# DeltaNet attention with a soft mixture of experts on one core: solved keys in feature-major form, the state product added to the solved values in PSUM, joins on 64-row tiles, 3 KB store rows, outputs transposed per step

## The chip, the cores and the metric

The kernel runs on one core of one Trainium2 chip. The metric is device time in microseconds (us), lower is better. The kernel before was timed three times: a median of 350.14 us, the lowest 349.73.

The engines are named as in the profile. PE is TensorE (matrix products and transposes), PEld its weight loads, DVE is VectorE, ACT is ScalarE, POOL is GpSimd, and SP is SyncE, which issues transfers only. A product of fp32 data appears as two matmul records, a transpose as one.

## The reference

There are 4 batches, 8 heads, 768 tokens and a head size of 48. The output of the delta rule is laid out as 3072 tokens of 384 features. It goes into a soft mixture of 8 experts with 4 slots each and a hidden size of 1024. All of it is fp32.

```python
k_n = k / (np.linalg.norm(k, axis=-1, keepdims=True) + 1e-06)
for t in range(S):
    y[:, :, t] = einsum('bhd,bhde->bhe', q[:, :, t], state)
    v_old = einsum('bhde,bhd->bhe', state, kt)
    state = state + bt[:, :, :, None] * einsum('bhd,bhe->bhde', kt, vt - v_old)
...
logits = x @ phi
d = exp(logits - logits.max(0));  d /= d.sum(0) + 1e-09
slot_input = d.T @ x
slot_out[e] = maximum(slot_input[e] @ w1[e], 0) @ w2[e]
c = exp(logits - logits.max(1));  c /= c.sum(1) + 1e-09
out = c @ slot_out
```

## The kernel before

The sequence is cut into 24 chunks of 32 tokens. The 4 batches times 32 tokens fill the 128 partitions, so one chunk covers all batches and heads. Four chunks make a group, of which there are six.

For each group, `invert(m)` builds the inverse of the 32 x 32 lower triangular matrix of every batch, head and chunk, scaled by beta and the key norms. DVE transposes the products of keys (`lb`, L509) and computes the norms (L524 to L540). The two diagonal 16 x 16 blocks are inverted by elimination (28 small steps, L558 and L562), on DVE for the first group and on POOL for the others. The off-diagonal block is joined by two series of small products on PE (X16, L601, and T16, L607). The result `DTb` is written in two copies masked by the parity of the batch.

For each chunk, `turn` transposes K and Q on PE (L446), and ACT copies the result to `X` (L455), keys in half 0 and queries in half 1. `products` forms K K' and Q K' (L473). They become `G` (for the inversion) and the masked `AT` (L494). `scale_v` multiplies V by the norms on POOL.

The recurrence is in `chain(n)`. It runs from the state St as follows:

- R: PE multiplies the keys with the state (L655), and DVE subtracts that from V into a tile R (L668).
- QS: PE multiplies the queries with the state (L655) into the bank of the output.
- W: PE applies the inverse to R (L678). DVE and ACT copy the solved values out in two masked halves (L689 and two at L694), and POOL adds the halves to `Wc` (L698).
- S: PE adds the update to the state, which stays in banks 6 and 7 (L706); ACT and DVE copy it to St (L716, L720).
- AU: PE multiplies AT with Wc and adds it to the output bank (L731); ACT copies it to Y (L737).

After each group, `route(m)` transposes the four chunks of Y (L755, one bank for each of three feature blocks), forms the logits, both softmaxes and the slot sums. After the last group, `experts()` forms the maximum over all tokens (L963), the slots' inputs (L981), the expert products (L1001 and L1039), and the output: 24 products of 384 columns (L1079), 12 copies of two banks each on DVE or ACT (L1086, L1089), and 48 stores with rows of 1.5 KB (L1096), from SP and ACT in turn. The weights are loaded into buffers of the recurrence as those become free.

The order of the work is written by `Plan` while the program is built. Each step is recorded with an engine, a cost, and what it reads and writes. `order()` then runs a list schedule by the longest remaining path and emits the steps engine by engine in that order. It counts the PSUM banks (six, of which four at most hold work outside the recurrence, kind "bulk") and puts products of the identity (fillers, `plan.fill`, L404) into gaps of PE. Each engine runs its instructions strictly in the emitted order. A transfer is issued by an instruction on SP, ACT or POOL and waits there until its buffer is free.

The constants are set before the first planned step: memsets of tS, Dn and St on POOL (L398 to L400), of the padding of K and Q on DVE (L397). The transfers of beta on POOL (L435) stand behind them.

Of the kernel before, what the change touches and what calls it, by code (L numbers as in the profile page):

```python
# [14 lines left out]

class Op:
    __slots__ = ("eng", "us", "fn", "deps", "succ", "acq", "rel", "bias", "land", "tail", "start", "end", "left", "at", "name", "area", "passes")
# [10 lines left out]
class Plan:  # L28
# [12 lines left out]
    WINDOW, KEEP, DENSE, BONUS, FORCE = 2.5, 0.46, 0.5, 40.0, 0.0  # L41

    def __init__(self, banks, limit):
# [3 lines left out]
        self.fill = None  # L47

    def op(self, eng, us, fn, r=(), w=(), acq=None, rel=None, pre=(), bias=0.0, land=0.0, name="", touch=None):
# [3 lines left out]
        o.eng, o.us, o.fn, o.acq, o.rel, o.bias, o.land, o.name = eng, us, fn, acq, rel, bias, land, name  # L53
# [50 lines left out]
    def order(self):  # L104
# [3 lines left out]
        clock, held = {}, {"bulk": 0, "chain": 0}  # L108
# [47 lines left out]
        while len(done) < n:  # L156
# [3 lines left out]
            for eng, ls in ready.items():  # L160
                now = clock.get(eng, 0.0)
                cand = []
                for t, o in ls:
# [10 lines left out]
                    if t is not None:  # L174
                        cand.append((t, o))
                if cand:
                    first = min(c[0] for c in cand)

                    def worth(c):
                        return c[1].tail + (bonus if eng == "PE" and c[1].area > self.DENSE * c[1].us  # L180
                                            else 0.0), -c[1].at
# [25 lines left out]
            if o.eng == "PE":  # L207
                idle = clock.get("PE", 0.0)
                while self.fill and idle >= self.fill[3] and (
# [8 lines left out]
                    f.eng, f.at, f.name, f.start = "PE", -1, "fill", idle  # L218
                    end = array(idle, self.fill[0], self.fill[1], 2)
                    f.us, idle, f.end = end - idle, end, end  # L220
                    t = max(t, idle)
                    done.append(f)
                    n += 1
                us = array(t, us, o.area, o.passes) - t
            o.start, o.end = t, t + us
# [27 lines left out]
def kernel(  # L253
# [16 lines left out]
    P = 128  # L270
# [32 lines left out]
    NK, NX, NV, NQ, NA = 11, 9, 7, 5, 9  # L303
# [10 lines left out]
    tt = buf([P, 2, QC, QC], "tt")  # L314
    pr = buf([P, 2 * 7 * 8], "pr")
    tS = buf([P, C, C], "tS")
    DT = buf([P, U, C], "DT")
    Gl = buf([P, U, QC], "Gl")
    DTb = ring(2, [P, U, 2, C], "DTb")
    tD, oD = buf([P, QC, 2, QC], "tD"), buf([P, U, QC], "oD")  # L320
    gmx = buf([P, 2, QC], "gmx")
    Dn = buf([P, U // 2, C], "Dn")
    X16 = buf([P, U // 2, 2, QC], "X16")
    R = buf([P, H, D], "R")
# [66 lines left out]
    nc.gpsimd.memset(low, -1.0)  # L391
    nc.gpsimd.affine_select(out=low, in_=low, compare_op=ALU.is_ge, fill=0.0, base=-1,
# [3 lines left out]
    for t in (Kall, Qall):  # L396
        nc.vector.memset(t.rearrange("p n (h d) -> p (n h) d", d=DP)[:, :, D:DP], 0.0)  # L397
# [762 lines left out]
```

## Time and profile before

| what | value |
|---|---|
| median of the runs | 350.14 us |
| the profiled execution's own time | 350.11 us |
| its span, first to last instruction | 348.3 us |
| instructions shown | 16203 |
| mean granted clock of TensorE | 0.931 |
| read from HBM, written | 39.47 MB, 4.72 MB |
| fillers (L404), matmul records | 232, 37.9 us busy |
| Wc on POOL (L698), 24 of 1002 ns | 24.0 us busy, 63.2 us idle ahead of it |
| key and query products with the state (L655), 1472 records | 37.5 us busy |
| solve (L678), 736 records on 64*64 tiles | 26.3 us busy |
| joins (L601 and L607), 768 records each on 32*32 tiles | 9.8 us busy each |

"Busy" is the time in which an engine had an instruction running. "Idle before" is the time it stood ahead of one, put down to what came last. PE's records overlap, so the mean of one record (220 ns for the solve) is longer than the distance from one to the next. The granted clock is the share of full speed that the throttle left to TensorE. All rows come from one execution, whose span is 1.8 us shorter than its own time.

### The profile page before, as it was taken

How to read it: one execution, taken by the hardware profiler on the slowest of the kernel's cores; microseconds unless marked ns; L12 is line 12 of the kernel's file. 1: busy time of each engine (PE TensorE's matmuls, PEld its weight loads, DVE VectorE, ACT ScalarE, POOL GpSimd, SP SyncE). 2: the span in 40 equal slices, each digit the busy share in tenths (PEclk: the TensorE clock that was granted, in tenths of full speed). 3: DMA queues.
4: the chain of work that ended last, by engine and by line, in shares of the span. 5: the costliest groups of instructions: out<-in, count | busy, mean ns of one | idle time of the engine just before them, and what ended most of it. 6: DMA issues, size and time to landing. Idle time of an engine off the chain costs nothing.

```text
span 348.3 us, 16203 instructions
## 1 busy us (share of the span) xinstructions
PE 278.8 (80%) x7182; PEld 222.1 (64%) x7182; DVE 178.4 (51%) x384; ACT 130.7 (38%) x258; POOL 132.0 (38%) x263
## 2 busy tenths in 40 slices
PE   2873096997959986898988878998787899999970
PEld 1762096886848776787867667886666787334430
DVE  7098919746561753836576484664642632210600
ACT  1321054543453625564436444453164434011050
POOL 9710401488128740289504891258811110000000
PEclk9987579998998999999899999999999999999955
DMA  6755643154445333324342405475458389697287
GB/s 120 134 85 91 100 67 59 28 88 81 75 106 86 66 55 70 66 49 77 52 80 77 111 10 145 110 193 164 135 173 332 104 272 307 212 389 282 75 259 208
DMA packets 90853, 45.24 MB, mean 130 GB/s; under 512 B 80400, under 2 KB 83600, under 8 KB 90784
## 3 DMA queue, kind: packets, MB, share of 16 engines
q1 hardware_dynamic: 74176, 39.15, 44.0%
q10 hardware_dynamic: 16064, 4.92, 6.5%
q8 instruction: 56, 0.92, 1.1%
q0 software_dynamic: 544, 0.15, 0.3%
q14 instruction: 13, 0.11, 0.1%
HBM read 39.47 MB, written 4.72 MB: 127 GB/s over the span
## 4 chain that ended last, share of the span: by engine, by line
PE 53%; POOL 17%; DVE 13%; issue 9%; DMA 3%; ACT 2%; SPq 0%; POOLq 0%; DVEq 0%; ACTq 0%
PE bank L655 6%; PE bank L731 6%; PE bank L446 5%; PE bank L678 5%; POOL tt L562 4%; PE bank L473 4%; POOL pr L558 4%; PE bank L404 4%; PE bank L1079 4%; PE bank L706 3%; PE bank L1039 3%; PE bank L1001 3%; POOL Wcall L698 3%; PE bank L601 3%; POOL bt L435 2%
## 5 line engine op out<-in xcount | busy, mean ns | idle before, releaser
L698 POOL TENSOR_TENSOR Wcall<-W 128x384 f32<-128x384 f32 x24 | 24.0, 1002 | 63.2 <-ACT W L694 59.1
L655 PE MATMUL bank<-St,X 128*32 128x96 f32 x1472 | 37.5, 248 | 8.6 <-issue 6.1
L455 ACT ACTIVATE X<-bank 128x1024 f32<-128x1024 f32 (+1 forms) x28 | 25.3, 902 | 42.2 <-PE bank L446 35.8
L404 PE MATMUL bank<-ident 128*128 128x128 f32 x232 | 37.9, 307 | 2.5 <-issue 2.5
L655 PEld LDWEIGHTS bank<-St,X 128*32 128x32 f32 x1472 | 31.1, 110 | 13.2 <-issue 8.8
L404 PEld LDWEIGHTS bank<-ident 128*128 128x128 f32 x232 | 32.8, 214 | 6.5 <-issue 4.8
L446 PE MATMUL bank<-ident,Kall 128*128 128x128 f32 x96 | 19.0, 331 | 20.9 <-DVE ATall L494 13.1
L473 PE MATMUL bank<-X 48*64 48x128 f32 (+1 forms) x896 | 28.4, 266 | 7.7 <-ACT X L455 3.4
L731 PE MATMUL bank<-Wcall,ATall 64*64 64x48 f32 x768 | 27.8, 221 | 8.3 <-POOL Wcall L698 6.9
L731 PEld LDWEIGHTS bank<-Wcall,ATall 64*64 64x64 f32 x768 | 24.8, 136 | 11.7 <-POOL Wcall L698 9.6
L694 ACT ACTIVATE W<-bank,par 128x192 f32<-128x192 f32 x48 | 17.6, 418 | 38.8 <-PE bank L678 28.4
L720 DVE TENSOR_TENSOR St<-bank,half 128x768 f32<-128x768 f32 x23 | 21.9, 952 | 19.3 <-PE bank L706 19.1
L473 PEld LDWEIGHTS bank<-X 48*64 48x64 f32 x896 | 23.3, 139 | 10.4 <-issue 5.1
L678 PE MATMUL bank<-R,DTb 64*64 64x48 f32 x736 | 26.3, 220 | 2.5 <-issue 1.4
L513 POOL TENSOR_TENSOR tt<-lb,low 128x256 f32<-128x256 f32 x12 | 8.5, 734 | 52.0 <-DVE lb L509 52.0
L446 PEld LDWEIGHTS bank<-ident,Kall 128*128 128x128 f32 x96 | 13.0, 168 | 24.0 <-DVE ATall L494 13.4
L678 PEld LDWEIGHTS bank<-R,DTb 64*64 64x64 f32 x736 | 23.6, 135 | 6.1 <-issue 3.6
L716 ACT ACTIVATE St<-bank 48x384 f32<-48x384 f32 x46 | 22.3, 484 | 13.3 <-PE bank L706 12.4
L562 POOL TENSOR_TENSOR tt<-tt,pr 128x28 f32<-128x28 f32 (+6 forms) x70 | 24.4, 348 | 5.5
L490 DVE SCALAR_TENSOR_TENSOR G<-bank,par,G 128x128 f32<-128x128 f32 x48 | 15.0, 344 | 20.8 <-ACT G L486 20.8
L558 POOL TENSOR_TENSOR pr<-tt 128x28 f32<-128x28 f32 (+6 forms) x70 | 23.7, 338 | 4.9
L689 DVE TENSOR_TENSOR W<-bank,par 128x384 f32<-128x384 f32 x24 | 13.3, 555 | 23.6 <-PE bank L678 23.4
(211 smaller groups left out, 533.6 us busy)
## 6 DMA issues: line engine op xcount, KB each, us to landing
Qall<-in_q_dram SPq DMA_DIRECT2D x96, 48.0 KB, 2.5
Kall<-in_k_dram SPq DMA_DIRECT2D x92, 48.0 KB, 2.4
X<-in_moe_w_dram SPq DMA_DIRECT2D x7, 512.0 KB, 4.2
X<-in_moe_w_dram SPq DMA_DIRECT2D x7, 384.0 KB, 6.4
Vall<-in_v_dram ACTq DMA_DIRECT2D x48, 48.0 KB, 2.7
Vall<-in_v_dram SPq DMA_DIRECT2D x48, 48.0 KB, 2.8
Kall<-in_moe_w_dram SPq DMA_DIRECT2D x4, 512.0 KB, 4.1
ATall<-in_moe_w_dram SPq DMA_DIRECT2D x3, 512.0 KB, 3.6
```

Source lines behind the costliest of these rows:

```text
L404: plan.fill = (0.223, 0.213, 0.1, 6.0, lambda b: nc.tensor.matmul(bank[:, b, 0:P], lhsT=ident, rhs=ident, start=True, stop=True, skip_grou ...
L446: nc.tensor.transpose(at(h, j)[:, P * e:P * e + P], src[:, P * e:P * e + P], ident)
L455: plan.op("ACT", act(512 * len(which)), lambda: nc.scalar.activation(dst, at(h, 0, 2) if len(which) > 1 else at(h).unsqueeze(1), ACT.Copy) ...
L473: nc.tensor.matmul(at(h, g)[rb, 2 * w * C * e:2 * w * C * (e + 1)], lhsT=x[r, 0, e, rb], rhs=x[r, which[0]:which[0] + w, e, rb], start=(e ...
L558: eng.tensor_tensor(o, t[:, :, j, 0:j].unsqueeze(2).broadcast_to([P, 2, w, j]), t[:, :, j + 1:QC, j].unsqueeze(3).broadcast_to([P, 2, w, j ...
L562: eng.tensor_tensor(t[:, :, j + 1:QC, 0:j], t[:, :, j + 1:QC, 0:j], o, op=ALU.add)
L655: nc.tensor.matmul(at(h)[rb, 2 * D * e:2 * D * e + 2 * D], lhsT=x[:, i, e, rb], rhs=St[:, b, e].rearrange("p g d -> p (g d)"), start=(e == ...
L678: nc.tensor.matmul(at(hw, u // HQ)[rb, D * (u % HQ):D * (u % HQ) + D], lhsT=t[rb, H * c + u].rearrange("p j t -> p (j t)"), rhs=rhs[rb, u, ...
L698: plan.op("POOL", pool(384), lambda: nc.gpsimd.tensor_tensor(wc, ww[:, :, 0, :], ww[:, :, 1, :], op=ALU.add), r=wk, w=[("Wc", n % 2)], nam ...
L716: plan.op("ACT", act(384), lambda r=r, g=g: nc.scalar.activation(St[r].rearrange("p (i j) e g d -> p i g (j e) d", i=2)[:, 0, g], bank[r, ...
L720: D_(dve(768, True), lambda: nc.vector.tensor_tensor(St.rearrange("p (i j) e g d -> p i (j e) g d", i=2)[:, 1], bank[:, SB + 1, 0:H * D].r ...
L731: nc.tensor.matmul(at(hy)[rb, D * u:D * u + D], lhsT=a[rb, u % 2, u // 2, :], rhs=wc[rb, u, :], start=(n == 0 and u == 0), stop=True, skip ...
```

## The change

The parts of the change, in the order of the kernel:

- Start: the memsets of tS, Dn, St, the padding and banks 6 and 7 become planned steps. Beta's transfers no longer stand behind them. All V loads are issued from SP instead of half of them from ACT. K has 10 ring slots instead of 11, V 6 instead of 7. The K half of `turn` and `products` stands apart from the Q half for the first three groups instead of the first.
- Inversion: the factor of the low triangle is formed from the norms (two DVE steps in place of two on POOL), tt has two buffers, and the norm is one step shorter (a factor of 2 is carried into V, a factor of 4 into beta, and taken out of Y by 0.5). The joins run as 32 products on 64-row tiles instead of 64 on 32-row tiles. For that Gl and Dn are written in two copies masked by parity (Gl by two ACT copies, Dn by two POOL steps).
- Recurrence: PE multiplies the inverse with the keys (KP), in feature-major form, and ACT copies it negated over the keys in X. VP applies the inverse to V itself. R multiplies the solved keys with the state and adds that to VP's result in the same banks. The subtraction on DVE and the tile R are gone. Wc is copied from PSUM by ACT instead of added on POOL.
- Routing: Y is transposed per chunk, three blocks into one bank.
- Output: cT is laid out by pairs of tokens, so that an output row in SBUF holds two neighbouring tokens (3 KB). 48 products of 64 rows replace 24 of 128. There are 24 stores; 18 are issued by SP, 6 by ACT. Four pairs of banks are used in turn, the last being the state's.
- Plan: a table of 150 priorities by engine and step, start times of the engines, and a cost for changing the tile shape on PE.

```diff
-    NK, NX, NV, NQ, NA = 11, 9, 7, 5, 9
+    NK, NX, NV, NQ, NA = 10, 9, 6, 5, 9
...
-        load(v, V[n % NV], ("V", n % NV), n, ("SP", "ACT"), [("V", n % NV)])
+        load(v, V[n % NV], ("V", n % NV), n, ("SP",), [("V", n % NV)])
...
+        for j in (1, 0):
+            plan.op("POOL", 0.72, lambda j=j: nc.gpsimd.tensor_tensor(
+                Dn[:, :, j, 0:QC], Dn[:, :, 0, 0:QC],
+                par[:, j:j + 1].unsqueeze(2).broadcast_to([P, U // 2, QC]), op=ALU.mult),
+                r=[kn], w=[kn], name="Dn2")
...
-        def couple(qs, first):
-            for q2 in qs:
-                for b in range(B):
-                    r = slice(C * b, C * b + C)
+        def couple(first):
+            for q2 in range(U // 2):
+                for i in range(2):
+                    r = slice(2 * C * i, 2 * C * i + 2 * C)
...
-            plan.op("PE", pe(16, 32, 96, 4, 0.25), lambda: state(hr, 0),
-                    r=[("X", n % NX, 0)] + sk, w=[hr], acq=hr, name="R")
-            D_(dve(384, True), lambda: nc.vector.tensor_tensor(
-                R.rearrange("p u d -> p (u d)"), vn.rearrange("p u d -> p (u d)"),
-                at(hr)[:, 0:Dm], op=ALU.subtract), r=[hr] + vk, w=["R"], rel=hr, name="R")
+            def solve_keys():
+                for e in range(HQ):
+                    for i in range(2):
+                        for g in range(2):
+                            rb = slice(2 * C * i, 2 * C * i + 2 * C)
+                            nc.tensor.matmul(
+                                at(hk, i)[DP * g:DP * g + DP, 2 * C * e:2 * C * e + 2 * C],
+                                lhsT=kk[rb, 2 * e + g, :],
+                                rhs=t[rb, H * c + 2 * e + g].rearrange("p j t -> p (j t)"),
+                                start=(e == 0), stop=True, skip_group_check=True)
+            plan.op("PE", pe(16, 64, 64, 4, 0.25), solve_keys,
+                    r=[("DTb", m % 2, j) for j in range(2)] + all4("K", n % NK), w=[hk], acq=hk,
+                    pre=[("X", n % NX, 0)], name="KP")
+            plan.op("ACT", act(512), lambda: nc.scalar.activation(
+                x[:, 0].rearrange("p e (i t) -> p i e t", i=2),
+                at(hk, 0, 2)[:, :, 0:2 * C * HQ].rearrange("p i (e t) -> p i e t", e=HQ), ACT.Copy,
+                scale=-1.0), r=[hk], w=[("X", n % NX, 0)], rel=hk, name="KP")
...
+            def shift():
+                for e in range(HQ):
+                    for b in range(B):
+                        rb = slice(C * b, C * b + C)
+                        e2 = 2 * D * (e % 2)
+                        nc.tensor.matmul(at(hw, e // 2)[rb, e2:e2 + 2 * D], lhsT=x[:, 0, e, rb],
+                                         rhs=St[:, b, e].rearrange("p g d -> p (g d)"),
+                                         start=False, stop=True, skip_group_check=True)
+            plan.op("PE", pe(16, 32, 96, 4, 0.25), shift,
+                    r=[("X", n % NX, 0)] + sk, w=[hw, "turns"], bias=LOOP, name="R")
...
-        plan.op("POOL", pool(384), lambda: nc.gpsimd.tensor_tensor(
-            wc, ww[:, :, 0, :], ww[:, :, 1, :], op=ALU.add), r=wk, w=[("Wc", n % 2)], name="Wc")
+        plan.op("ACT", act(384), lambda: nc.scalar.activation(
+            wc.rearrange("p (i u) d -> p i (u d)", i=2), at(hw, 0, 2)[:, :, 0:HQ * D], ACT.Copy),
+            r=[hw], w=[("Wc", n % 2)], rel=hw, name="Wc")
...
+            def product(m=m, ii=ii):
+                for qt in range(2):
+                    for c in range(GC):
+                        r = slice(C * c, C * c + C)
+                        half_ = slice(DP * (c % 2), DP * (c % 2) + DP)
+                        nc.tensor.matmul(two(ii[c // 2])[half_, qt, 0:Dm], lhsT=cT[r, m, qt, :],
+                                         rhs=so[r], start=True, stop=True, skip_group_check=True)
...
+                    dst = out.rearrange("(b n t q) f -> n t b q f", b=B, n=NS, q=2)[
+                        GC * m + 2 * s + x].rearrange("t b q f -> t b (q f)")
+                    on = "ACT" if x and s else "SP"
```

More of the change, by code (lines that the diff above doesn't have):

```diff
@@ L861, in weights @@
         home(["tS"], flat(tS), 1024)
+        for i in range(2):
+            home([("tt", i), ("tt1", i), ("tD", i)], flat(tt[i]), 1024)
+            home([("gl", i), ("tD", i)], flat(gl[i]), 1024)
         home(["DT"], flat(DT), 1024)
@@ L1109 @@
             load_small()
+        if apart:
+            for n in ns:
+                turn(n, (0,))
+                products(n, (0,))
             for n in ns:
@@ L1113 @@
             load_v(n)
-        for n in ns:
-            if m:
+        if not apart:
+            for n in ns:
                 turn(n, (0, 1))
                 products(n, (0, 1))
-            else:
-                turn(n, (0,))
-                products(n, (0,))
         invert(m)
+        if m == 0:
+            plan.mark = ""
         for n in ns:
-            if m == 0:
+            if apart:
                 turn(n, (1,))
```

347 lines of the change are left out of this document (200 added, 147 removed), and 15 rows, old and new, of the table BIAS.

## The prediction

> **What bounds the kernel now.** I read the page first, then a table of stretches, then the chain of waits in order of time, then TensorE's instructions one by one.
>
> ```profile
> PE 278.8 (80%) x7182; PEld 222.1 (64%) x7182; DVE 178.4 (51%) x384; ACT 130.7 (38%) x258; POOL 132.0 (38%) x263
> ...
> q8 instruction: 56, 0.92, 1.1%
> ...
> PE 53%; POOL 17%; DVE 13%; issue 9%; DMA 3%; ACT 2%; SPq 0%; POOLq 0%; DVEq 0%; ACTq 0%
> ```
>
> PE leads the chain, but POOL holds 17% of it and "issue", time in which PE waited for nothing the profile shows, 9%. The table splits the span at the first solve (62.58), at the maximum over the tokens (293.30), at the first expert product and at the first output product. Its columns are the stretch, its length, then busy us of PE, PEld, DVE, ACT and POOL, the granted clock, DMA share and GB/s. The single line under it is the same table for the fillers alone (L404, products of the identity that compute nothing).
>
> ```profile
> 0.00:62.58 62.58, 35.69 (x742) 31.91 (x744) 40.70 (x103) 17.18 (x28) 21.59 (x45) 0.84 0.53 92
> 62.58:293.30 230.72, 199.59 (x6113) 171.95 (x6113) 125.18 (x254) 104.70 (x215) 110.00 (x217) 0.98 0.47 113
> 293.30:297.70 4.40, 4.05 (x31) 2.60 (x30) 3.09 (x14) 1.24 (x5) 0.40 (x1) 1.00 0.94 371
> 297.70:325.35 27.65, 27.30 (x253) 10.63 (x254) 4.14 (x7) 2.85 (x5) 0.00 (x0) 1.00 0.70 260
> 325.35:348.30 22.95, 12.17 (x48) 4.99 (x48) 5.28 (x6) 4.75 (x6) 0.00 (x0) 0.63 0.71 206
> ```
>
> ```profile
> 62.58:293.30 230.72, 23.46 (x154) 20.45 (x154) 0.98 0.47 113
> ```
>
> So the recurrence takes 230.7 us, of which PE works usefully 199.6 - 23.5 = 176.1; 54.6 us are fillers or idle. The chain says what the rest waits for:
>
> ```profile
> 5.47 8.36 POOL bt L435 x15
> 13.83 3.96 DMA bt<-in_beta_dram
> ...
> 22.33 2.00 DVE lb L509
> ...
> 42.74 5.79 PE bank L446 x28
> ...
> 57.27 2.49 issue
> ...
> 62.58 0.62 PE bank L678 x16
> ...
> 79.19 0.97 POOL Wcall L698
> ...
> 325.35 12.19 PE bank L1079 x48
> ```
>
> The first inversion starts at 22.33 because beta's 16 transfers are issued behind POOL's constants. It has DT and Dn ready at 42.0, but the solve starts only at 62.58, since 28 transposes, products and a 2.49 us issue wait stand ahead. At 79.19 PE waits for the sum Wc, which stood on POOL behind 13 us of elimination. The issue waits have a pattern:
>
> ```profile
> 133.35 0.67 PE L731 MATMUL bank<-Wcall,ATall 64*64 64x48 f32 x16 [1.25 <-issue]
> 133.95 0.75 PE L607 MATMUL bank<-X,Dn 32*32 32x32 f32 x64
> 134.64 1.20 PE L655 MATMUL bank<-St,X 128*32 128x96 f32 x48
> 137.36 0.54 PE L655 MATMUL bank<-St,X 128*32 128x96 f32 x16 [1.52 <-issue]
> ```
>
> Between two such waits lie 16+64+48 = 128 matmul records in 4.01 us. Each has a weight load: 256 instructions. Queue 8 moved 0.92 MB in 56 packets, 16.4 KB each, and 2 x 7182 / 56 is 256.5. I read this as code that arrives in blocks of 256 instructions, at best one per 4.0 us. PE is thus bound twice: by work, and by records per time.
>
> **The change part by part.** Counts are from the instruction streams of the two built programs, durations from the rows above and the page.
>
> *Start.* Beta's transfers go ahead of POOL's memsets of tS (0.95), Dn (0.53) and St (1.38); only the select of low (0.51) stands between the first and the other 15: first issue near 2.4 instead of 5.4, last done near 11.9, landed 3.96 later, 15.8; beta was copied at 17.91. The three memsets follow and are needed only by the tS writes, Dn and the first state product, 20 us later. Four G halves (0.30 each) and a reciprocal (0.35) follow it on DVE, so lb starts near 17.6 instead of 22.33. ACT issues no V loads any more (its first X waited until 8.4 behind eight of them), and the products of K1 and K2 stand behind K3's transposes, whose last piece lands near 10.3 (SP's twelfth issue ended at 7.9, 2.4 to landing); the four are done near 16. From lb: 2.0; the norm 2.0; the low products and N 1.6; four G halves 1.2 and nT 0.2: 24.6. Elimination was 8.35 (27.95 to 36.3), with four more G halves 1.2: 34.2. tS 1.4, DT 1.92: 37.5. The join now stands directly behind on PE: 1.4 to 2.1. Beside it tD, oD, Dn (2.4) and two new POOL scalings of Dn (0.7 each, by the 0.73 of a tS half): 41.4. The second join, its subtraction 0.69, DTb 1.14, hops: first solve near 46.3 (44 to 50), against 62.58. That gains 16 us. What stood in between goes into PE's idle time during elimination (nine K products instead of four) or into the recurrence, where I count it.
>
> *Recurrence, PE work.* From 176.1: solved keys, 23 groups of 32 records. Not in the trace; nearest is the 64x64 product, 0.56 by weight loads to 0.69 by busy time a group, so 0.62: +14.3. Joins: ten of 64 records on 64*64 instead of 128 on 32*32. The old took about 1.4. The new costs 2.1 by L678 (64*64, 32 records in 1.06, 48 columns), or 1.4 if time goes with its 32 columns; I take the middle, +3.5 (0 to +7). Products split in two for groups 1 and 2: 14 narrow and 12 wide against 1 and 16, 13 x 0.62 - 4 x 0.98 = +4.1. Transposes 140 against 112, 0.13 each: +3.6. Sum 201.6. The state product accumulated into the solve's bank counts as before, 0.74; there is no row for a product that adds to what lies in PSUM, bounds 0.6 to 1.1 (L678).
>
> *Recurrence, what falls away.* The loop from solve to solve where little else runs was 6.12 us (278.72 to 284.84). DVE's R (0.55) and the solve (1.06) leave it, with their hops about 1.9. As PE has over 8 us of work per chunk, this pays only in that waits can be filled. Wc moves to ACT (24 of 0.49 by the Y row of the same size), R leaves DVE (12.7), V loads leave ACT. ACT gains 23 key copies of 0.60 and six Gl of 0.63: its 104.7 becomes some 135 in 222 us. Fillers fall from 154 records to 4, so 23.5 us leave.
>
> *Recurrence, idle.* Idle was 31.1. PE's issue waits, summed over its lines, are 15 without the fillers at the start. Records rise from 6113 to 6367 (49.7 blocks; 199 us at 4.0), but the densest bursts, the joins, halve. I keep 15 and add 5 for waits that the new order meets: 201.6 + 20 = 222 (207 to 240). Two waits are new. VP waits for the KP copy on ACT; behind it stand R, the update and the next chunk. In the issued order S, AU, transposes or logits stand between KP and VP nearly everywhere, 0.8 to 1.1 against 0.6 and a hop, so I count nothing; uncovered it costs 0.7 a chunk, 16 in all. And all 48 V loads that ACT issued move to SP (0.47 each, 22 us), on rings one shorter for K and V: one that waits for its slot holds K, Q and weights behind it. PE waited 3.0 for a K load once (105.06); 0 to 6, inside the 5. A gain would need waits on V that PE does not show.
> [...]
>
> *Tail.* 4.4 as before. Experts 27.65; weights have less time to come in, and DMA share there is 0.70 already: 28.5 (27 to 31). Output was 22.95: one side evacuated first (DVE six in a row, 0.87 apart), ACT's last stores were issued at 345.0. Now 24 stores of 3 KB rows instead of 48, 18 of them on SP, and both engines alternate. PE's 48 quarter products should take the old 24's 12.2 (8 to 16, by the clock); then evacuation 0.95, issue 0.5, landing 2.7; 4.72 MB at the 300 GB/s of such slices is 16: 19 (16 to 23).
>
> Sum: 46.3 + 222 + 4.4 + 28.5 + 19 = 320.2; outside the span lie 350.1 - 348.3 = 1.8, and the profiled execution's 350.11 is the median, 350.14. **322 us.**
>
> **The rivals.**
> *Code arrival paces everything.* If blocks keep the old mean, 230.7 / 47.8 = 4.83 us, the recurrence takes 49.7 x 4.83 = 240, the total 340. For it: more records, the dense KP. Against: the old mean holds fillers and POOL's waits.
> *Code hidden.* Idle 5 instead of 20: 307. Against: the fence above; for: the joins made the largest waits, and they halve.
> [...]
> *Row tiles that share a bank run in turn.* Output products of chunks 0 and 1 now write halves of one bank. If they alternate, two run at a time as before, on twice the records: 24.4 instead of 12.2, and with the 4.2 behind them 28.6 instead of 19: 332. Against: L678's two row tiles write one bank, and 33 ns a record is less than 48 columns alone take (L655's 64 records of 96 columns take 1.46 us on four tiles: 46 ns for 48 columns on one).
> [...]
> *ACT becomes the loop.* St's copies (0.97) stand in order behind Wc (0.49), KP (0.60) and at times X (1.03) or Gl (1.25), 1.1 to 3.4 us against the 0.81 that the update covers. If St comes 1.5 us late in each of 23 chunks and PE has nothing ordered before the next state product, 34.5 us are added: 357, slower from there; at 2 us, 368, what I take for this case. For it: ACT is strictly in order. Against: 135 of 222 us busy, and VP, KP, QS and AU of neighbouring chunks stand ahead of the next state product.
>
> **How the numbers follow.** Forecast 0.68 (own range 308 to 336), code paced 0.10, code hidden 0.10, bank 0.05, ACT 0.07. The range 305 to 341 takes in all but ACT's case and the ends. Two per cent, 7.0 us, is about what a measurement of this kernel can tell from no change: faster is below 343.1, slower above 357.1. Faster: 0.66 + 0.06 + 0.10 + 0.05 = 0.87; same 0.07; slower 0.06.
>
> **What would show it.** First solve (the VP line) near 46; lb near 17.6; nothing of Wc on POOL; fillers some 70 records in all; KP near 0.6 a group, a join 1.4 to 2.1; first solve to the maximum 222; last output product to the end under 5. Wrong if ACT copies end PE's waits, if issue waits grow beyond 15 us, or if the start stays above 50.

## The result, and the profile after

The changed kernel takes 322.72 us (median of four runs, 322.18 to 326.84), the kernel before 350.16 us beside it (349.73 to 358.49): a ratio of 0.9246, 95% interval 0.9149 to 0.9342. The profiled execution of the changed kernel has a span of 320.4 us.

From the page of the changed kernel, the lines that answer to those of before: busy time of the engines, the queue that the page names instruction, and the shares of the chain that ended last.

```profile
PE 273.6 (85%) x7296; PEld 223.1 (70%) x7296; DVE 167.0 (52%) x363; ACT 156.5 (49%) x325; POOL 107.0 (33%) x239
...
q8 instruction: 57, 0.93, 1.2%
...
PE 61%; DVE 14%; POOL 7%; issue 5%; DMA 5%; ACT 4%; SPq 0%; ACTq 0%; DVEq 0%; POOLq 0%
```

POOL's share of the chain fell from 17% to 7%. Of what is left, some 8 us are the issue of beta's transfers and another 8 us steps of the elimination; Wc is gone from it. The table of stretches, split at the same places as before: first solve (now VP, 43.10), maximum over the tokens, first expert product, first output product. Columns are the stretch, its length, then busy us of PE, PEld, DVE, ACT and POOL, the granted clock, DMA share and GB/s.

```profile
0.00:43.10 43.10, 30.09 (x563) 26.98 (x563) 37.20 (x99) 15.38 (x30) 20.14 (x43) 0.92 0.57 96
43.10:269.40 226.30, 206.83 (x6367) 180.14 (x6367) 116.58 (x238) 131.75 (x280) 86.09 (x194) 0.96 0.54 128
269.40:273.90 4.50, 3.92 (x31) 2.49 (x31) 3.31 (x15) 1.53 (x6) 0.80 (x2) 1.00 0.80 316
273.90:299.20 25.30, 24.44 (x245) 9.81 (x245) 4.13 (x7) 2.98 (x5) 0.00 (x0) 1.00 0.62 235
299.20:320.40 21.20, 8.33 (x96) 3.72 (x96) 5.75 (x6) 4.86 (x6) 0.00 (x0) 0.80 0.70 223
```

The fillers alone (L466 now) take 0.61 us in the second stretch:

```profile
43.10:269.40 226.30, 0.61 (x4) 0.53 (x4) 0.96 0.54 128
```

Against before: the start is 19.5 us shorter, the recurrence 4.4, the experts 2.35, the output 1.75; the stretch of the maximum is 0.1 longer. Inside the recurrence much more moved than its length shows. PE's useful work rose from 176.1 to 206.83 - 0.61 = 206.2, by 30 us; fillers and idle time together fell from 54.6 to 20.1. A stretch that hardly changes can hide an exchange of this size, so "busy" has to be read with the fillers taken out.

The chain in order of time shows the new start: beta lands at 14.4 and lb begins at 16.21 (before 22.33), the first solve's stretch follows at 43.10. At the end the experts' products run in three unbroken blocks; before, the two series of products alternated with the transposes between them, and ten fillers stood among and behind them.

```profile
11.13 3.28 DMA bt<-in_beta_dram
...
16.21 1.96 DVE lb L574
...
32.97 1.90 DVE DT L670
...
273.88 10.51 PE bank L1118 x96
...
284.38 2.10 PE bank L1137 x16
...
286.49 10.50 PE bank L1156 x128
```

What PE waited for inside the recurrence (engine, line, releaser, us in total, times, longest), first the four largest of before, then the seven largest of 23 now:

```profile
PE bank L731 <- POOL Wcall L698: 6.9, 9, 2.1
PE bank L655 <- issue: 6.1, 6, 1.6
PE bank L607 <- issue: 4.2, 3, 1.8
PE bank L446 <- DMA Kall<-in_k_dram: 3.0, 1, 3.0
```

```profile
PE bank L508 <- DMA Kall<-in_k_dram: 2.2, 2, 1.8
PE bank L706 <- issue: 2.1, 2, 1.3
PE bank L817 <- issue: 1.9, 3, 0.8
PE bank L743 <- issue: 1.6, 3, 0.9
PE bank L701 <- issue: 1.4, 1, 1.4
PE bank L508 <- DMA Qall<-in_q_dram: 1.4, 1, 1.4
PE bank L508 <- ACT Wcall L808: 1.2, 1, 1.2
```

Nothing large is left: issue waits are 9.6 us over all lines (14.9 before), loads of K and Q 3.6, and no wait on ACT, whose busy time rose from 104.7 to 131.75, is over 1.2.

### The profile page after: what moved, and what is told of

Its sections match the earlier page's. It is cut to its first block, busy times and chain, and to the rows that moved or that the text cites. A ratio compares the mean times of both kernels' runs of the same rounds, so it can differ in the third digit from the quotient of the medians.

```text
span 320.4 us, 16406 instructions
## 1 busy us (share of the span) xinstructions
PE 273.6 (85%) x7296; PEld 223.1 (70%) x7296; DVE 167.0 (52%) x363; ACT 156.5 (49%) x325; POOL 107.0 (33%) x239
## 3 DMA queue, kind: packets, MB, share of 16 engines
HBM read 39.47 MB, written 4.72 MB: 138 GB/s over the span
## 4 chain that ended last, share of the span: by engine, by line
PE 61%; DVE 14%; POOL 7%; issue 5%; DMA 5%; ACT 4%; SPq 0%; ACTq 0%; DVEq 0%; POOLq 0%
PE bank L842 7%; PE bank L536 6%; PE bank L743 5%; PE bank L773 5%; PE bank L817 5%; PE bank L787 5%; PE bank L508 4%; PE bank L755 3%; PE bank L1118 3%; PE bank L1156 3%; PE bank L701 3%; PE bank L706 3%; POOL bt L497 3%; PE bank L866 2%; DVE DT L670 2%
## 5 line engine op out<-in xcount | busy, mean ns | idle before, releaser
L518 ACT ACTIVATE X<-bank 128x512 f32<-128x512 f32 (+1 forms) x36 | 25.9, 739 | 32.1 <-PE bank L508 32.1
L725 POOL TENSOR_TENSOR Vall<-Vall,nT 128x384 f32<-128x384 f32 x24 | 19.8, 830 | 61.5 <-DMA Vall<-in_v_dram 29.9
L536 PE MATMUL bank<-X 48*64 48x64 f32 (+1 forms) x1152 | 32.9, 258 | 5.7 <-ACT X L518 5.3
L827 ACT ACTIVATE St<-bank 48x384 f32<-48x384 f32 x46 | 22.3, 484 | 22.1 <-PE bank L817 12.9
L773 PE MATMUL bank<-Vall,DTb 64*64 64x48 f32 x768 | 28.0, 222 | 0.6 <-issue 0.5
L773 PEld LDWEIGHTS bank<-Vall,DTb 64*64 64x64 f32 x768 | 25.6, 138 | 3.2 <-issue 1.2
L657 POOL TENSOR_TENSOR tt<-tt,prPOOL 128x28 f32<-128x28 f32 (+6 forms) x70 | 24.7, 353 | 5.2
L804 ACT ACTIVATE W<-bank,par 128x192 f32<-128x192 f32 x48 | 17.5, 416 | 18.2 <-PE bank L787 17.4
L653 POOL TENSOR_TENSOR prPOOL<-tt 128x28 f32<-128x28 f32 (+6 forms) x70 | 23.7, 339 | 5.0
L817 PE MATMUL bank<-W,Kall 64*48 64x96 f32 x736 | 22.6, 251 | 2.5 <-issue 1.9
L817 PEld LDWEIGHTS bank<-W,Kall 64*48 64x48 f32 x736 | 17.5, 123 | 5.1 <-issue 3.4
L557 DVE TENSOR_TENSOR ATall<-bank,tri 128x512 f32<-128x512 f32 x24 | 16.4, 685 | 8.5 <-PE bank L536 8.1
```

The lines of the kernel that those rows point to most:

```text
L518: plan.op("ACT", act(512 * len(which)), lambda: nc.scalar.activation(dst, at(h, 0, 2) if len(which) > 1 else at(h).unsqueeze(1), ACT.Copy) ...
L536: nc.tensor.matmul(at(h, g)[rb, 2 * w * C * e:2 * w * C * (e + 1)], lhsT=x[r, 0, e, rb], rhs=x[r, which[0]:which[0] + w, e, rb], start=(e ...
L653: eng.tensor_tensor(o, t[:, :, j, 0:j].unsqueeze(2).broadcast_to([P, 2, w, j]), t[:, :, j + 1:QC, j].unsqueeze(3).broadcast_to([P, 2, w, j ...
L657: eng.tensor_tensor(t[:, :, j + 1:QC, 0:j], t[:, :, j + 1:QC, 0:j], o, op=ALU.add)
L773: nc.tensor.matmul(at(hw, u // HQ)[rb, D * (u % HQ):D * (u % HQ) + D], lhsT=t[rb, H * c + u].rearrange("p j t -> p (j t)"), rhs=vn[rb, u, ...
L817: nc.tensor.matmul(bank[DP * g:DP * g + D, SB + i, 0:H * D].rearrange("p (j e d) -> p e j d", j=2, e=HQ)[:, e], lhsT=kk[r, 2 * e + g, 0:D] ...
```

## The experiments

Several parts came together, so each experiment undoes one part of the changed kernel or makes one part in the kernel before. A row of this table is one profiled execution up to the maximum over the tokens, after which each takes another 51 to 58 us. "Work" is PE's busy time less the fillers, "rest" what is left of the time. The ratio is to the kernel before on the same chip.

| kernel | median us, ratio [95%] | first solve | maximum | work | rest | clock of the recurrence |
|---|---|---|---|---|---|---|
| before | 350.16 | 62.6 | 293.3 | 200.7 | 92.6 | 0.98 |
| changed | 322.72, 0.9246 [0.9149, 0.9342] | 43.1 | 269.4 | 226.6 | 42.8 | 0.96 |
| changed, no priorities | 338.77, 0.9679 [0.9593, 0.9764] | 50.4 | 285.3 | 232.9 | 52.4 | 0.96 |
| changed, joins on 32 rows | 333.15, 0.9526 [0.9474, 0.9578] | 43.3 | 274.1 | 222.7 | 51.4 | 0.96 |
| changed, Wc on POOL | 335.82, 0.9522 [0.9439, 0.9606] | 43.1 | 284.5 | 232.0 | 52.5 | 0.94 |
| changed, old output | 324.31, 0.925 [0.9166, 0.9334] | 45.4 | 272.4 | 227.5 | 44.9 | 0.98 |
| before, beta first | 347.83, 0.998 [0.9922, 1.0038] | 60.3 | 291.2 | 201.9 | 89.3 | 0.97 |
| before, whole start | 347.67, 0.9943 [0.99, 0.9986] | 50.7 | 290.8 | 221.0 | 69.8 | 0.92 |
| before, Wc on ACT | 354.26, 1.0125 [1.0062, 1.0189] | 61.9 | 296.2 | 206.1 | 90.1 | 0.95 |
| before, new step | 385.4, 1.0928 [1.0788, 1.1068] | 63.8 | 329.1 | 230.7 | 98.4 | 0.92 |
| before, no fillers | 363.37, 1.04 [1.0322, 1.0478] | 60.0 | 302.5 | 231.0 | 71.5 | 0.89 |
| changed, old step, own priorities | 314.82, 0.8998 [0.893, 0.9066] | 53.0 | 261.9 | 218.7 | 43.2 | 0.97 |

In three rows the profiled execution is not the usual one. With joins on 32 rows it took 326.92 us, and the next one 330.69; the two are 0.93 and 0.94 of the 351.23 us that the kernel before took on that chip, and the ratio in the table is nearer to the three longer runs. With Wc on POOL it took 337.84, where two others took 332.01 and 334.58, and with the new step 386.02, where two others took 379.14 and 384.78. In these two rows, then, small differences in work and rest prove nothing.

**The start alone.** In the kernel before:

```diff
-    nc.gpsimd.memset(tS, 0.0)
-    nc.gpsimd.memset(Dn, 0.0)
-    nc.gpsimd.memset(St, 0.0)
+    plan.op("POOL", 0.95, lambda: nc.gpsimd.memset(tS, 0.0), w=["tS"], name="zero")
+    plan.op("POOL", 0.53, lambda: nc.gpsimd.memset(Dn, 0.0), w=["Dn"], name="zero")
+    plan.op("POOL", 1.38, lambda: nc.gpsimd.memset(St, 0.0), w=[("St", i) for i in range(3)],
+            name="zero")
```

> The kernel before with one part of the change: the memsets of tS, Dn and St on POOL are planned steps behind beta's 16 transfers. Theory A (the start is a chain through beta): lb starts near 19.4 instead of 22.33, and since 28 transposes still stand between, the first solve gains only what beta gains, 2.9; total 347. Theory B (the solve waits for PE's queue of transposes and products, not for the inversion): first solve unchanged at 62 to 63, total 350. Theory C (it gains the whole 16 to 19 us): total 332 to 335.

The first solve moved by 2.3 us and the maximum by 2.1, and lb starts at 19.34, theory A; the ratio of the times cannot tell 2 us from none. Then with V's loads on SP and the K halves first as well:

```diff
-        load(v, V[n % NV], ("V", n % NV), n, ("SP", "ACT"), [("V", n % NV)])
+        load(v, V[n % NV], ("V", n % NV), n, ("SP",), [("V", n % NV)])
...
-            if m:
+            if m > 2:
                 load_q(n)
...
+        if m < 3:
+            for n in ns:
+                turn(n, (0,))
+                products(n, (0,))
             for n in ns:
                 load_q(n)
```

> The kernel before with the start parts of the change together: memsets behind beta's transfers, V loads on SP alone, the K halves of the first three groups' transposes ahead of their Q halves. Theory A (the start's gain of 19.5 us lies in these parts and the rest is independent): first solve at 44 to 50, total 331 to 336, less whatever the Q halves cost that move into the recurrence (3 to 6 us). Theory B (without the priorities the transposes still stand ahead of the first solve): first solve at 57 to 62, total 345 to 350.

The two windows of this kernel up to the maximum:

```profile
0.00:50.70 50.70, 29.45 (x704) 24.62 (x705) 40.45 (x106) 16.78 (x32) 25.85 (x59) 0.72 0.55 92
50.70:290.80 240.10, 206.42 (x6287) 177.84 (x6287) 125.13 (x251) 105.99 (x220) 104.70 (x204) 0.92 0.47 113
```

The total is theory B's, the first solve is not: it comes 11.9 us earlier, but the recurrence grows by 9.4, from 230.7 to 240.1, and the total gains only 2.5 us. Its fillers there fell to 13.83 us, so PE worked 192.6 us instead of 176.1, at a clock of 0.92 instead of 0.98. Two causes lie in that and are not told apart. An estimate that lets PE's time go inversely with the clock makes 176.1 into 176.1 x 0.98 / 0.92 = 187.6 us, most of the growth; the remaining 5 us would be work, some of it moved, some of it new (products split in two). What the clock does to one step is seen in the kernel before: four transposes (L446) took 0.60 us at 27.87, at a clock of 1.00, and 1.06 at 44.50, at 0.50. Either way an earlier start is not worth its length by itself: the recurrence has to take the work that used to stand ahead of it, and the clock has to hold.

**The new step alone.** In the kernel before, KP, its copy, VP on V and R added in PSUM take the place of R, DVE's subtraction and the solve; all else, Wc on POOL too, as before:

```diff
-            plan.op("PE", pe(16, 32, 96, 4, 0.25), lambda: state(hr, 0),
...
-            D_(dve(384, True), lambda: nc.vector.tensor_tensor(
...
+            plan.op("PE", pe(16, 64, 64, 4, 0.25), solve_keys,
...
+            plan.op("ACT", act(512), lambda: nc.scalar.activation(
...
+            plan.op("PE", pe(16, 32, 96, 4, 0.25), shift,
```

> The kernel before with one part of the change: the new recurrence step (KP, its copy by ACT, VP on V, R added in PSUM), Wc still on POOL, old start, joins and output, no priorities. Theory A (the old loop leaves 54.6 us of waits and fillers, and the shorter loop lets PE fill them): in spite of 14.3 us more work the stretch falls to 215 to 225, total 334 to 345. Theory B (the new step is an exchange: what PE's loop wins in waits it pays in work and code): stretch 228 to 240, total 348 to 360.

```profile
0.00:63.80 63.80, 35.73 (x766) 31.95 (x768) 41.16 (x103) 17.16 (x28) 21.29 (x45) 0.84 0.52 89
63.80:329.10 265.30, 216.49 (x6749) 184.64 (x6739) 114.47 (x232) 118.08 (x238) 109.34 (x217) 0.92 0.41 102
```

Worse than theory B: the recurrence takes 265.3 us instead of 230.7, and the kernel is 9.3% slower. PE works 30 us more (206.6 without 9.86 us of fillers; KP is 14.3 of it, and the clock fell from 0.98 to 0.92), and fillers and idle time stay, 58.7 us against 54.6. The part that carries the change's name is, put alone, a loss. The planner's order is another here too, and it is not a better one: PE waits 7.4 us for DVE's DT (0.9 before). So the run shows that the step does not pay by itself in this planner's order, not that it could not in another.

**The old step in the changed kernel.** The same edit undone, all else as changed.

> The changed kernel with the old recurrence step: no KP and no copy of it, R into a bank of its own, V minus R on DVE, then the solve. Everything else as changed (start, joins, Wc on ACT, output, priorities). PE has 14.3 us less work and 11.5 blocks less code in the stretch; the loop from state to state is 1.9 us longer. Theory A (PE's work and code bind, the loop is covered by other work): stretch 226 minus 10 to 14, total 308 to 313. Theory B (the loop binds as soon as it has DVE and the solve in it): idle time and fillers come back as in the kernel before (54.6 us), stretch 235 to 245, total 330 to 342.

Median 326.87 us (324.66 to 328.52 without the profiled execution, which took 337.53 at a mean clock of 0.884 and is left out of the table), ratio 0.9318, 95% interval 0.9239 to 0.9397: between the two theories, and no worse than the changed kernel as far as the intervals tell, though its priorities were made for the new step. So they were searched again for the old one:

> The changed kernel with the old recurrence step, as in the run of that name before, but with a table of priorities searched anew for it with the planner's own estimate as the objective, until that estimate was as good as the changed kernel's. Theory A (KP's work of 14.3 us and its 11.5 blocks of code are not worth the shorter loop once the order is fitted): total 308 to 318. Theory B (both forms are worth the same, work against waits): 319 to 326. Theory C (the loop through DVE binds whatever the order): 327 or more.

```profile
0.00:53.00 53.00, 34.67 (x622) 30.74 (x622) 43.39 (x112) 20.12 (x37) 28.16 (x65) 0.71 0.56 93
53.00:261.90 208.90, 187.60 (x5526) 164.20 (x5525) 124.29 (x248) 115.00 (x249) 79.31 (x173) 0.97 0.55 136
```

314.82 us, theory A, and the fastest kernel here: its interval lies below the changed kernel's. The start is 10 us longer (PE does 33.7 us of work ahead of the first solve instead of 20.3, at a clock of 0.71), but the recurrence is 17.4 us shorter: 185.1 us of work instead of 206.2, 841 records fewer, and 21.3 us idle instead of 19.5. DVE's R, which is back in the loop, ended only 1.1 us of PE's waits in the recurrence. Up to the maximum the rest is the same as in the changed kernel, 43.2 us against 42.8, and the 7.5 us that are won are work, 218.7 against 226.6: without KP the waits did not come back. Whether another table would give the new step as much was not tried, so the run compares two orders as well as two steps.

**The order.** The table of priorities emptied:

```diff
-BIAS = {
-    "ACT.DTb": 1.7, "ACT.DTb0": 0.8, "ACT.DTb5": -9.4, "ACT.G": 105.2, "ACT.G0": -5.0,
...
-}
+BIAS = {}
```

> The changed kernel with its table of priorities emptied, so the list schedule orders by the longest path alone. Theory (the order fills PE's waits): PE's work in the stretch from the first solve to the maximum stays near 206, its idle time rises from 19.5 towards 35, the first solve comes at 45 to 50 instead of 43.1; total 335 to 345. Rival (the order is set by work alone and the table is fine tuning): total 319 to 327.

```profile
50.40:285.30 234.90, 206.38 (x6302) 180.35 (x6303) 114.48 (x229) 131.31 (x279) 85.50 (x189) 0.96 0.51 127
```

The total is as the theory had it: 338.77, 16 us more. The first solve is 7.3 us later and the recurrence 8.6 longer (234.9), the experts 2.8. PE's work stays at 205.1 and its idle time rises to 28.5, not quite to 35. Together with the fillers that is 29.8 us, against 20.1 with the table and 54.6 in the kernel before. So the table is worth more than half of the gain, but most of the waits of before are gone without it; the planner's other changes (start times, the cost of a change of tile shape) are still in this run and were not taken out by themselves.

**Wc.** First back on POOL in the changed kernel, then moved to ACT in the kernel before:

```diff
-        plan.op("ACT", act(384), lambda: nc.scalar.activation(
-            wc.rearrange("p (i u) d -> p i (u d)", i=2), at(hw, 0, 2)[:, :, 0:HQ * D], ACT.Copy),
-            r=[hw], w=[("Wc", n % 2)], rel=hw, name="Wc")
+        plan.op("POOL", pool(384), lambda: nc.gpsimd.tensor_tensor(
+            wc, ww[:, :, 0, :], ww[:, :, 1, :], op=ALU.add), r=wk, w=[("Wc", n % 2)], name="Wc")
```

> The changed kernel with Wc added up on POOL again (1.0 us, 24 times) instead of copied by ACT (0.49 us). Theory (AU is off the loop and the plan knows POOL's cost): PE's chain takes at most a few waits for Wc, total 322 to 326. Rival (POOL's eliminations in front of Wc hold AU and the output bank as in the kernel before): PE waits for Wc behind eliminations, total 329 to 336.

> The kernel before with one part of the change: Wc copied from PSUM by ACT (0.49 us) instead of added on POOL (1.00 us). PE waited 6.9 us for Wc from POOL in the stretch of before, and POOL's eliminations no longer stand ahead of it. Theory A (the waits for Wc were real and the time behind them is not taken by anything else): stretch 218 to 224, total 337 to 344. Theory B (the loop through R, DVE and the solve, or the late start, sets the stretch of before): fillers take the place of the waits, total 347 to 351.

On POOL the changed kernel takes 335.82, its two shortest runs 332.01 and 334.58, the rival's number. PE's waits in the recurrence then name POOL, and issue waits at the same line:

```profile
PE bank L841 <- issue: 5.6, 2, 3.8
PE bank L841 <- POOL Wcall L808: 4.3, 4, 2.0
PE bank L743 <- issue: 3.9, 3, 1.9
```

The rival's mechanism is seen only in part: the waits for Wc are 4.3 of the 15.1 us by which the recurrence is longer. Issue waits are 14.2 instead of 9.6, work 211.7 instead of 206.2, fillers 4.29 instead of 0.61, and the order is planned anew.

In the kernel before the same move makes it 1.25% slower, which neither theory had: the waits for Wc are gone, but the planner now writes another order, in which PE waits 8.4 us for DVE's DT (L582; 0.9 before) and has 84 fillers instead of 154 at a clock of 0.95:

```profile
PE bank L601 <- DVE DT L582: 8.4, 4, 2.7
```

A single edit in a kernel whose order is planned is not the edit alone.

**Fillers.** The kernel before with `plan.fill = None`:

> The kernel before without its 232 records of fillers. Theory A (fillers only occupy time in which PE waits anyway, and they are no cost to be won): total 348 to 352, the 37.9 us turn up as idle time. Theory B (fillers push work back and take code blocks): total 325 to 345. Theory C (they hold the granted clock up): clock below 0.9, total 355 or more.

```profile
0.00:60.00 60.00, 34.07 (x752) 27.96 (x754) 41.77 (x108) 18.91 (x31) 22.13 (x47) 0.91 0.58 98
60.00:302.50 242.50, 196.90 (x5900) 167.36 (x5892) 124.03 (x250) 102.89 (x213) 109.34 (x216) 0.89 0.45 110
```

363.37 us, 4% slower, nearest to theory C: the clock of the recurrence falls from 0.98 to 0.89, and PE's work there grows from 176.1 to 196.9, by 12%; an estimate by the ratio of the clocks, 0.98 / 0.89, gives 10%. Fillers are not free: up to the maximum the rest falls from 92.6 to 71.5 us without them. But PE's work rises from 200.7 to 231.0, by more than the rest falls. The order differs from before's too (742 records ahead of the first solve in before, 60 of them fillers, and 752 here), so not all of this is the clock. That the fillers held the clock up is a reading of this pair of runs. An idle PE and a low clock do stand together in the kernel before: PE ran nothing from 29.85 to 42.74, and the clock was 0.50 from 31 on. The small kernel below shows no such thing: its clock is 1.00, with waits of up to 4.59 us.

**Joins and code.** The joins on 32-row tiles, at the same planned cost, so in the same order:

```diff
-                for i in range(2):
-                    r = slice(2 * C * i, 2 * C * i + 2 * C)
+                for b in range(B):
+                    r = slice(C * b, C * b + C)
...
-                                         lhsT=Gl[r, q2].rearrange("p j x -> p (j x)"),
+                                         lhsT=Gl[r, q2, b % 2, :],
```

> The changed kernel with the joins as 64 products on 32-row tiles (128 matmul records each) instead of 32 on 64-row tiles, with the same planned cost, so the same order. Six more blocks of 256 instructions in all. Theory A (work bounds PE where it is busy, code arrives in time): each join costs 1.4 us instead of 1.84 to 2.17, 12 joins save 6 us, total 315 to 318. Theory B (code arrival bounds it): a join's 128 records come no faster than one block in 3.4 to 4.0 us and the stretch grows by 5 blocks of 4.55, total 330 to 345, with issue waits at the lines of the joins or right behind them. In between (323 to 328): the burst drains what had been fetched, and the waits behind it eat the saved work.

The profiled execution took 326.92, the case in between; the four others took 330.7 to 333.9, theory B's number. In the profiled one PE's work in the recurrence falls by 4.2 us, as theory A said in kind, but the recurrence grows by 4.5, and issue waits explain it, 22.1 us instead of 9.6:

```profile
PE bank L787 <- issue: 6.9, 4, 3.6
PE bank L706 <- issue: 6.6, 5, 2.6
PE bank L743 <- issue: 2.3, 3, 1.1
PE bank L701 <- issue: 2.1, 3, 0.9
```

So five more blocks of 256 instructions (queue 8 moved 63 packets over the span instead of 57) came with 8.7 us more of idle time, twice what the smaller work saves. The longest wait, 3.6 us at 225.91, stands where the expert weights come in at 340 GB/s. A kernel of its own measured this apart, with products so small that a block of them takes 1.89 us. These are the lines of it that count:

```python
        small(64 * 16, a)
        small(4, gate)
        nc.sync.dma_start(out=gate, in_=moe_w1[0, 0:P, 0:64])
        for n in range(24):
            eng = nc.sync
            eng.dma_start(out=w1[:, n], in_=moe_w1[n // 3, P * (n % 3):P * (n % 3) + P, :])
...
        small(64 * 16, a)
        small(64 * 4, w2[:, 3, 7])
```

> A kernel of its own that leaves out the whole computation and writes zeros: PE runs 1024 products on 32-row tiles with 8 columns (2048 matmul records, 16 blocks of 256 instructions) with no transfers beside them, then the same with 19 MB of weight loads beside them, then 256 more. Theory A (code arrives in blocks): 128 records take 3.4 to 4.0 us in the quiet part, though the joins' 128 records on such tiles take 1.4 us of work, with an issue wait once in each block; and longer, 4.5 us or more, beside the loads. Theory B (code is hidden): 128 records take 1.4 us or less in both, no issue waits.

Its chain in order of time (start, us, what), first without transfers, then beside transfers of about 400 GB/s (the weight loads, then the stores of the zeros), which end near 123, and behind them:

```profile
0.98 3.16 PE bank L49 x223
4.14 1.61 issue
5.75 1.89 PE bank L49 x128
7.64 1.57 issue
9.21 1.89 PE bank L49 x128
11.09 2.12 issue
...
94.03 1.89 PE bank L49 x128
95.91 4.58 issue
100.50 1.89 PE bank L49 x128
102.39 4.31 issue
...
126.89 1.84 issue
128.74 1.88 PE bank L49 x128
```

Theory A, sharper than expected: PE stops after every 128 products' records, 256 instructions with their weight loads, for 1.56 to 2.12 us without transfers and 4.31 to 4.59 beside them. A block comes every 3.46 to 4.01 us without transfers (14 blocks from 9.21 to 62.50, mean 3.81), and every 6.2 to 6.5 us beside the transfers (7 blocks from 68.70 to 113.16, mean 6.35). So half of the time goes into waiting between blocks, and 70% beside the transfers. These products are far quicker to run than those of the kernel, whose recurrence takes 4.55 us a block; that PE waits for blocks there too is read from the joins above, not from this kernel.

**The output.** The changed kernel with the old products, evacuations and 48 stores with rows of 1.5 KB:

```diff
-                        nc.tensor.matmul(two(ii[c // 2])[half_, qt, 0:Dm], lhsT=cT[r, m, qt, :],
+                        nc.tensor.matmul(at(h, b)[:, 0:Dm], lhsT=cT[r, m, :], rhs=so[r],
...
-                for x in range(2):
-                    dst = out.rearrange("(b n t q) f -> n t b q f", b=B, n=NS, q=2)[
...
+                for b in range(B):
+                    dst = out[b * S:(b + 1) * S].rearrange("(n t) f -> t n f", t=C)[
```

> The changed kernel with the old output part: 24 products of 128 rows, 48 stores with rows of 1.5 KB. Theory A (bytes bind: 4.72 MB at about 300 GB/s either way): the output takes 21 to 23 us from the first product, total 322 to 325. Theory B (rows of 1.5 KB are slower per byte): output over 25 us, total 327 or more.

Theory A: 324.31 against 322.72, intervals nearly the same, and the output takes 22.3 us instead of 21.2. In the changed kernel the last 21.4 us, in 40 slices, look like this:

```profile
DMA  0000000599999999998999898989899899878100
GB/s 0 0 0 0 0 0 0 161 195 327 293 207 276 350 356 333 333 293 316 299 339 241 241 362 299 327 299 270 264 356 333 287 333 253 218 281 316 63 0 0
```

From the first to the last byte the DMA engines are busy at nine tenths and move some 300 GB/s, so PE does not decide here. The row size does not tell in the total, but it is not without effect: in the middle of the stores, over ten us, rows of 3 KB move 313 GB/s (306 to 316), and over a slice of their page, 308.3 to 316.4, rows of 1.5 KB move 266. Over the whole output it is 223 and 212.

## Why the prediction was right, and where it was not

The total was 322 us against 322.72, and the span 320.2 against 320.4. What the prediction said would happen did: an earlier first solve, and a recurrence in which waits and fillers give way to more work. That the number is so close is luck: against the sum, the start came 3.2 us early, the recurrence 4.3 late, the experts 3.2 early and the output 2.2 late. And two readings of the cause need correction.

- **Start**, 46.3 predicted (44 to 50), 43.1 measured, just below its range. The chain through beta was right; each link ran slightly early (beta landed at 14.4 instead of 15.8, lb began at 16.21 instead of 17.6).
- **"That gains 16 us."** As a gap in time this is right, as a cause it is not. The same parts in the kernel before bring the first solve 11.9 us forward and the total 2.5. The step booked the start as a gain of its own; the recurrence had to take the moved work and the clock had to hold, and that depends on the other parts: on the table of priorities (without it 16 us are lost), and on others that the runs do not separate. The prediction never priced the table by itself. Part of its effect, the counts of records and fillers, it read from the built instruction streams, and these counts came out.
- **Work of the recurrence**, 201.6 predicted, 206.2 measured. The joins were mis-sized: the middle of 1.4 and 2.1 us was taken, and 64 records in one piece take 1.84 to 2.21, that is 29 to 35 ns a record beside the 33 of the 48-column solve. Fewer columns gave little or nothing back; for ten joins that is 1 to 5 us more than was booked. An estimate by the ratio of the clocks would explain the difference as well: 201.6 x 0.98 / 0.96 = 205.8. The two are not told apart. KP takes 0.62 us a group as estimated, and the accumulating product R 0.80, the same as QS beside it, inside its bounds of 0.6 to 1.1.
- **Idle time of the recurrence**, 20 predicted, 19.5 measured by another sum: issue waits 9.6 instead of 15, K and Q loads 3.6, single waits for engines for the rest. Halved joins are a reason for fewer issue waits; on 32 rows they are 22.1 us. Nothing followed from the KP wait: the cover named for it was there.
- **The loop from solve to solve.** The prediction took DVE's R and the solve out of it, some 1.9 us a chunk with their hops, and said that this pays only where the waits can be filled. The runs do not show that it pays: alone the new step leaves fillers and idle time where they were (58.7 us against 54.6), and with the old step and its own order the rest is no larger than in the changed kernel (43.2 against 42.8). So the fall of the waits came, but the shorter loop is not shown to be its cause.
- **"Fillers fall from 154 records to 4, so 23.5 us leave."** The count was right, the saving is not. Taken out by themselves from the kernel before, fillers save nothing and the time is 4% longer. In the changed kernel the clock stays at 0.96 with four of them, while PE is busy for 206.83 of 226.30 us.
- **Experts**, 28.5 predicted, 25.3 measured. The expectation that the weights would hold them up was wrong: the products run unbroken, 10.51, 2.10 and 10.50 us, at a DMA share of 0.62.
- **Output**, 19 predicted, 21.2 measured; "last output product to the end under 5" is wrong, it is 12.8 us (307.65 to 320.4). The step took PE's quarter products at 12.2 us and let the stores follow them. PE needs 8.33, and the stores set the end: first bytes at 302.9, then 4.72 MB at 300 GB/s.
- **Rivals.** Bank: ruled out, 96 records in 8.33 us with two row tiles writing halves of one bank. Code hidden: ruled out, idle time is 19.5 us instead of 5, 9.6 of it issue waits, and with five more blocks they were 22.1 us. Code paces everything: not at 4.83 us, the recurrence took 226.3 / 49.7 = 4.55 us a block, above the 3.81 that the small kernel needs without transfers, and PE's issue waits are 9.6 us; but by these numbers the blocks are a near bound, above all while weights come in (from 219.0 to 269.4 the kernel ran 1275 records, 5.06 us a block, at 251 GB/s). ACT becomes the loop: did not happen, its largest single entry in PE's waits is 1.2 us.

What the forecast could not see is that the new recurrence step is not shown to earn its place. Alone it costs 9%; under the same priorities the old step takes as long as far as the intervals tell, and with priorities of its own it is 8 us faster. Of the other parts, undoing the priorities in the changed kernel costs 16 us, undoing Wc 10 to 13, undoing the joins 4 to 10, undoing the output nothing that can be told. These do not add up to shares of the 27 us, because each edit also changes what the others are worth: Wc on ACT is a gain here and a small loss in the kernel before. Undoing the start inside the changed kernel was not tried, so how much of its 19.5 us the new order could do without stays open. Nor was a table of priorities made for the kernel before, so what the order alone would give there is open too.

## What to carry to other kernels

Split a large change and put its parts alone both ways, into the kernel before and out of the kernel after: here the part that names the change was a loss alone and no loss to take out, and the order of the steps was worth more than any other part that was undone. A gain ahead of a loop counts only as far as the loop has room for the work that is moved into it. That room is PE's time less its work; fillers belong to the room, but before they are taken out or filled with work, look at what the granted clock will be (0.89 without them here, 0.98 with them). Count instructions as well as work on TensorE, above all where weights are loaded beside it: in the small kernel 256 instructions came every 3.81 us, and every 6.35 beside transfers.

## What the runs showed of the hardware

- In the small kernel TensorE stopped after every 256 instructions. A block came in 3.46 to 4.01 us without transfers and in 6.2 to 6.5 us beside transfers of 400 GB/s, two thirds longer in the mean. That these are blocks of code is read from queue 8, which moved 35 packets, 0.57 MB, for 4616 matmul records and as many weight loads, 264 instructions a packet.
- Its first 223 records ran in one piece, in 3.16 us; behind them PE waited at every block, for 1.56 us at the least.
- The granted clock of the recurrence fell from 0.98 to 0.89 when fillers were left out, and work took 12% longer, in another order; an estimate by the ratio of the clocks gives 10%.
- R, which is added to what lies in PSUM, and QS, which starts anew, both took 0.80 us for 32 records (the median of the 16 whole groups of each on the chain that ended last), with a median of 246 ns a record.
- Stores of 4.72 MB moved 313 GB/s in the middle with rows of 3 KB and 266 with rows of 1.5 KB; the output took 21.2 and 22.3 us.
